# In the second batch, a pair's reciprocals copied in two parts, and the sums of w2's blocks placed behind masks and tallies

## The chip, the cores and the metric

The kernel runs on one core of one Trainium2 chip. The metric is device microseconds from start to end of one execution; the median of several runs is given. A profiled execution gives the trace from which all durations here are read.

## The reference, cut to what matters

Four batches of 768 positions. First comes attention of 8 heads of 64, in which a query sees only the keys whose six sign bits of a random projection agree with its own:

```python
q_bits = (einsum('bhsd,dk->bhsk', q, proj) > 0)      # and k_bits; a bucket number from six bits
mask   = q_bucket[..., None] == k_bucket[..., None, :]
scores = where(mask, scale * q @ k.T, -1e9)
attn   = softmax(scores);  x = attn @ v               # heads side by side: (4, 768, 512)
X = real(fft(fft(x, axis=1), axis=2));  u = x + X
un = (u - mean(u)) / sqrt(var(u) + 1e-6)
out = u + relu(un @ w_ch1) @ w_ch2                    # 512 -> 2048 -> 512
```

The weights come as 64-bit floats and are narrowed to 32 bits on the chip.

## The kernel before

The work is tiled by batch (b = 0 to 3). A batch has four pairs of heads; n counts pairs, so batch 1 has pairs 4 to 7. Each pair is done in six visits, one for each chunk c of 128 keys. In a visit, PE computes the chunk's scores in two halves of queries (L905, in two PSUM buffers that take turns), ACT exponentiates each half (`weights`, L916), DVE multiplies both heads by the 0/1 mask (`weigh`, L930, two instructions) and adds the chunk to a running sum (`tally`, L1020, one instruction in batch 1), and one visit later PE multiplies by v (`values`, L941). After a pair's last chunk `scale` divides: PE adds the tallies over keys (L960), DVE transposes the sums (L967), adds a small number and takes the reciprocal (L969, L970); ACT copies the reciprocals from 32-partition blocks into place, eight copies of 32x12 (L976); DVE transposes them out over the positions (L977) and multiplies x (L981). The generator `scale` stops (`yield`) after L970, and `attention` resumes it at the same visit or the next.

Beside the attention of batch b goes the rest of batch b - 1, as a second generator that `_main` advances between visits: `mix` (the Fourier part by folded matrices: `fold` L1099 to L1117, L1139, L1168, L1182) and then `mlp7`. The channel network is computed by a seven-product scheme on quarters of the matrices. Its inner part, for f = 0 to 7 in two halves, has seven products each (L1447); ACT copies or activates their PSUM banks (L1469, L1472, L1476, L1479, L1484, L1488, L1496, and L1486, L1490, L1498 in SBUF), DVE adds (L1473, L1480, L1485, L1489, L1497). Its outer part, `outer7`, once after each half, takes three pairs of row tiles with seven products each (L1326), whose banks are freed by DVE (L1338, L1372) or ACT (L1345, L1356, L1359). DVE prepares its left sides (L1311, L1312, L1346, L1354). Two PSUM banks in turn serve all these products, the bits (L836), the transposes (L1194) and the pairs' sums (L960).

In batch 0's channel network the weights are also still being made. `weights2` brings w2 in 16 slices, eight for each half of the network: a DMA on GpSimd's queue (L704), then `narrow`: DVE L639 and L643, ACT L647, L654, L655, DVE L652 twice. After each second slice DVE makes four sums of w2's blocks, each 128x256 (L1292 to L1295), which the outer products use beside the slices; SyncE's queue stores all seven blocks to DRAM (L1297) for later batches. For w1 the like is done by `quarters` (L1241 to L1244, stores at L1246 and L1247). SyncE's queue also carries the loads of q, k and v (L562, L568, L576) and of stored blocks (L1331, L1420).

The order on each engine is made by a scheduler from the program's order of tracing, with priorities and a model of times; it fixes each engine's queue at build time. Two tools in the code bend it: `behind()` puts a PE instruction behind a named one with higher priority, and `in_turn()` (a context of `_main`) puts all instructions traced inside it behind the instructions last noted in `done_by`, one for each engine. Noted are, for DVE, the masks L930, L1182 and some adds of the inner part, and for ACT the exponentials L916, L1146 and some of the inner part's copies. The conversion `arrival.convert` runs inside `in_turn()`, as does the tallying of batches 2 and 3 (`n >= TWO`, TWO = 8). The loop of visits for batches 0 and 1 is this, in short:

```python
new = chunk(c, scores(n, c)); tally(c, new[2], new[4])
for sc in scales: next(sc, None)          # then scales.clear()
while pending: finish()                   # values; after chunk 5, scale() up to its yield
for sc in scales if b else (): next(sc, None)
pending.append(new)
```

Of the kernel before, what the change touches and what calls it, by code (L numbers as in the profile page):

```python
# [17 lines left out]
ALU = mybir.AluOpType  # L18
# [8 lines left out]
NPAIR = H // 2  # L27
# [458 lines left out]
def _main(  # L486
# [13 lines left out]
    nc = tc.nc  # L500
# [13 lines left out]
    def wt(shape, dtype, tag, name, bufs=2):  # L514
        return work.tile(shape, dtype, tag=tag, name=name, bufs=bufs)
# [4 lines left out]
    def pt(shape, name):  # L520

        turn[0] += 1
        if roomy[0] and turn[0] % 2:
            if turn[0] % 4 == 1:
                return ps_o.tile(shape, F32, tag="o", name=name)
            return ps_sc.tile(shape, F32, tag="sc", name=name)
        return ps_1.tile(shape, F32, tag="ps", name=name)
# [152 lines left out]
    ET = mybir.EngineType  # L680
    done_by = {}

    @contextmanager
    def in_turn():

        with ExitStack() as st:
            for ins in done_by.values():
                st.enter_context(tc.issue_after(ins.ins))
            yield
# [186 lines left out]
    @contextmanager  # L876
    def behind():

        with tc.issue_after(last[0].ins), tc.high_priority(offset=AHEAD):
            yield  # L880

    TWO = 8
# [53 lines left out]
    def values(n, c, pk, oos):  # L936

        for g in range(2):
            w = HALF + 1 - g
            for h in range(2):  # L940
                oo = nc.tensor.matmul(  # L941
                    oos[g][h * D : (h + 1) * D, 0:w], nat["v", n][:, (2 * c + h) * D : (2 * c + h + 1) * D],
                    pk[:, g, h, 0:w], start=(c == 0), stop=(c == NT - 1),
                )
        last[0] = oo

    def scale(n, oos, sums):


        x = xs[n // NPAIR][:, n % NPAIR]  # L950
        vs = wt([P, 1], F32, "vs", f"vs{n}")
        nc.scalar.copy(vs, oos[0][:, HALF : HALF + 1])
        halves = [x[:, g * HALF : (g + 1) * HALF] for g in range(2)]
        for g, xg in enumerate(halves):
            nc.scalar.activation(xg, oos[g][:, 0:HALF], AF.Identity, bias=vs)

        ps = pt([P, HALF], f"sum{n}")
        for i, part in enumerate(sums):
            for j in range(4):
                nc.tensor.matmul(  # L960
                    ps[32 * j : 32 * j + 32, :], ones, part[:, j // 2, j % 2],
                    start=(i == 0), stop=(i == len(sums) - 1),
                )


        rt = wt([P, S], F32, "rt", f"rt{n}", 1)
        nc.vector.transpose(rt[:, 0:HALF], ps)  # L967
        rc = wt([P, HALF // 32], F32, "rc", f"rc{n}")
        nc.vector.tensor_scalar(rc, rt[:, 0:HALF:32], S * EPS, None, op0=ALU.add)  # L969
        nc.vector.reciprocal(rc, rc)  # L970
        yield
        rr = wt([P, 2, HALF // 32], F32, "rr", f"rr{n}")
        for g in range(2):
            for i in range(4):
                j = 2 * g + i // 2
                nc.scalar.copy(rr[32 * i : 32 * i + 32, g], rc[32 * j : 32 * j + 32])  # L976
        nc.vector.transpose(  # L977
            rt.rearrange("p (j i) -> p j i", i=32),
            rr.rearrange("p g j -> p (g j)")[:, :, None].broadcast_to([P, S // 32, 32]),
        )  # L980
        nc.vector.tensor_tensor(x, x, rt, op=ALU.mult)  # L981

    def attention(b):
        xs[b] = wt([P, NPAIR, S], F32, "x", f"x{b}")
        pending, scales = [], []

        def finish():
            n, c, pk, oos, sums = pending.pop(0)
            with behind() if n >= NPAIR and t is not None else nullcontext():
                values(n, c, pk, oos)  # L990
            if c == NT - 1:
                scales.append(scale(n, oos, sums))
                next(scales[-1])

        for t in range(NPAIR):
            n = NPAIR * b + t
            half = fold(b, 0) if t == NPAIR - 1 else iter(())
            if 1 < n + 1 < NPAIR * B:
                load(n + 1)
            ahead = prepare(n + 1) if n + 1 < NPAIR * B else iter(())  # L1000
            oos = [ps_o.tile([P, 512], F32, tag="o", name=f"oo{n}_{g}") for g in range(2)]
            acc = wt([P, 2, 2, HALF], F32, "acc", f"acc{n}", 1)
            first = None
            def chunk(c, pss):

                return n, c, weigh(n, c, pss), oos, [acc]

            def tally(c, pk, sums):

                nonlocal first  # L1010
                new = pk[:, :, :, 0:HALF]
                if c == 0:
                    first = new
                elif c == NT - 1 and b == 0:

                    sums.append(new)
                else:

                    for g in (0, 1) if b == 0 else (slice(0, 2),):
                        nc.vector.tensor_tensor(  # L1020
                            acc[:, g], (first if c == 1 else acc)[:, g], new[:, g],
                            op=ALU.add,
                        )

            for c in range(NT):
                if n < TWO:
                    new = chunk(c, scores(n, c))
                    tally(c, new[2], new[4])

                    for sc in scales:  # L1030
                        next(sc, None)
                    scales.clear()
                    while pending:
                        finish()
                    for sc in scales if b else ():
                        next(sc, None)
                    pending.append(new)
                elif c % 2 == 0:
                    pss = scores(n, c)
                    if len(pending) > 1:  # L1040
                        finish()
                    new = [chunk(c, pss)]
                    if pending:
                        finish()
                    new.append(chunk(c + 1, scores(n, c + 1, True)))
                    for sc in scales:
                        next(sc, None)
                    scales.clear()
                    pending += new
                else:  # L1050
                    with in_turn():
                        for p in pending:
                            tally(p[1], p[2], p[4])
                if c > (3 if b == 1 else 2):
                    next(half, None)
                if c > 0:
                    next(ahead, None)
                yield
        t = None
        while pending:  # L1060
            finish()
        for sc in scales:
            next(sc, None)


    HW = HALF // 2
# [199 lines left out]
    def weights2():  # L1266

        slices = []
        for half in range(2):
            for r in range(HF // 2):  # L1270
                for hi, first in ((0, B11), (1, B21)):
                    c = half * HF // 2 + r + hi * HF

                    step = 1 if hi else T1 - B11
                    dst = w2f[:, 0 : 7 * QB].rearrange("p (i r n) -> p i r n", i=7, n=HD)
                    slices.append(
                        (dst[:, first : first + step + 1 : step, r],
                         moe_w_ch2[c * P : (c + 1) * P, :])
                    )
        arrival = Arrival(slices, [zt2[:, i] for i in range(2)], NDC * DFF // WC, nc.gpsimd)  # L1280
        for half in range(2):
            if half == 0:
                for i in range(arrival.depth):
                    arrival.fetch(i)
                yield
            for i in range(HF):
                with in_turn():
                    arrival.convert(half * HF + i)
                yield
                if i % 2:  # L1290
                    b11, b21, b22, t4, t1, t2, t3 = (q[:, i // 2] for q in right7)
                    nc.vector.tensor_tensor(t3, b22, t1, op=ALU.subtract)  # L1292
                    nc.vector.tensor_tensor(t1, t1, b11, op=ALU.subtract)
                    nc.vector.tensor_tensor(t2, b22, t1, op=ALU.subtract)
                    nc.vector.tensor_tensor(t4, b21, t2, op=ALU.subtract)  # L1295
            for i in range(7):
                nc.sync.dma_start(bd[half, i], right7[i])  # L1297
            if half == 0:
                yield
# [350 lines left out]
```

## Time and profile before

| what | us |
|---|---|
| median of 3 runs | 1080.63 (1079.46 to 1081.03) |
| the profiled execution | 1081.91 |
| its span, first to last instruction | 1080.1 |
| PE busy | 1036.7 |
| DVE busy | 789.2 |
| ACT busy | 500.4 |
| exponentials L916, 192 of 809 ns | 147.4 busy |
| masks L930, 132 of 1014 ns | 128.7 busy |
| tallies L1020, 72 of 1485 ns on average | 106.0 busy |
| reciprocal copies L976, 128 of 198 ns (median) | 25 (128 x 0.198) |

The profiled execution's time is larger than its span by what lies ahead of the first and after the last instruction. In the trace's lines, the number in front is the start in us from the span's start, then the duration, the engine, the line of the kernel, the operation, what it writes and reads (buffer numbers left out), and shapes; the bracket at the end is the time in which the engine was idle before it and what ended that. A line can stand for several equal instructions that follow each other. PE's matmuls overlap, so a busy PE is not one at its peak; idle time of an engine that isn't the slowest costs nothing by itself. A stage is a stretch of the span for which the busy time of each engine was asked.

### The profile page before, as it was taken

To read this page: it belongs to the slowest core of one execution; us is meant where nothing else is said; L and a number is where in the kernel's file an instruction comes from. 1 tells how busy PE (TensorE), PEld (TensorE's weight loads), DVE (VectorE), ACT (ScalarE), POOL (GpSimd) and SP (SyncE) were. 2 spreads that over 40 slices of the span, in tenths; PEclk is the share of its full clock that TensorE was granted. 3 is DMA by queue.
4 is the path that set the end of the run, shared out by engine and by line. 5 is a ranking of instruction groups with operands and counts; after the bars stand their busy time and mean duration, and the time that the engine had idled before them with its cause. 6 is when DMAs were issued, how large, how long until landed. Compare 5 with 4: busy or idle time off the path is not lost.

```text
span 1080.1 us, 14131 instructions
## 1 busy us (share of the span) xinstructions
PE 1036.7 (96%) x4933; PEld 633.0 (59%) x4933; DVE 789.2 (73%) x1336; ACT 500.4 (46%) x1055; POOL 59.1 (5%) x132
## 2 busy tenths in 40 slices
PE   7989898999999999999999999999999999999997
PEld 3333354447644585545664576645675579668576
DVE  5899969888599977767857876776856875644353
ACT  6988554762277324455326424354315522440420
POOL 0000000002000020010000020010000012100000
PEclk9999899999999999999999999999999999999999
DMA  9654452390056271224062233222033205122301
GB/s 215 190 141 77 85 141 71 115 250 2 3 136 216 95 211 28 52 64 88 6 187 76 69 90 130 49 64 69 15 105 100 69 20 175 60 79 87 128 20 42
DMA packets 175710, 103.13 MB, mean 95 GB/s; under 512 B 129552, under 2 KB 162960, under 8 KB 175632
## 3 DMA queue, kind: packets, MB, share of 16 engines
q1 hardware_dynamic: 169840, 88.65, 30.5%
q0 software_dynamic: 4224, 13.11, 3.9%
q8 instruction: 41, 0.67, 0.3%
q10 hardware_dynamic: 1568, 0.39, 0.2%
q14 instruction: 37, 0.30, 0.1%
HBM read 81.14 MB, written 20.97 MB: 95 GB/s over the span
## 4 chain that ended last, share of the span: by engine, by line
PE 71%; DVE 17%; ACT 6%; issue 3%; SPq 2%; DMA 1%; DVEq 0%; ACTq 0%
PE o L1326 26%; PE h_p L1447 21%; PE oo L941 8%; PE sc L905 8%; DVE acc L1020 3%; DVE pk L930 3%; PE cs L1139 2%; PE A L1168 2%; ACT pk L916 2%; PE B L1168 1%; SPq L576 1%; DMA kn<-in_k_dram 1%; ACT rr L976 1%; DVE x L1182 1%; DVE w L643 1%
## 5 line engine op out<-in xcount | busy, mean ns | idle before, releaser
L1326 PE MATMUL o<-w,h 128*128 128x256 f32 x1152 | 258.4, 381 | 1.6 <-ACT tq L1345 0.9
L1326 PEld LDWEIGHTS o<-w,h 128*128 128x128 f32 x1152 | 216.7, 190 | 42.0 <-issue 6.4
L916 ACT ACTIVATE pk<-sc 128x768 f32<-128x768 f32 x192 | 147.4, 809 | 80.7 <-PE oo L941 33.2
L1447 PE MATMUL h_p<-x,w 128*128 128x384 f32 x448 | 164.1, 494 | 0.8 <-DVE rt L967 0.4
L905 PE MATMUL sc<-qt,kt 64*128 64x384 f32 x768 | 155.9, 508 | 3.6 <-ACT pk L916 3.3
L930 DVE SCALAR_TENSOR_TENSOR pk<-qb,kb,pk 128x768 f32<-128x768 bf16 x132 | 128.7, 1014 | 32.6 <-ACT pk L916 32.5
L941 PE MATMUL oo<-pk,vn 128*64 128x385 f32 (+1 forms) x768 | 146.8, 495 | 2.6 <-DVE pk L930 2.0
L1447 PEld LDWEIGHTS h_p<-x,w 128*128 128x128 f32 x448 | 82.0, 190 | 66.7 <-issue 9.9
L1020 DVE TENSOR_TENSOR acc<-acc,pk 128x1536 f32<-128x1536 f32 (+1 forms) x72 | 106.0, 1485 | 5.3 <-ACT pk L916 5.1
L1447 PE MATMUL h_p<-w 128*128 128x384 f32 x288 | 106.1, 490 | 0.1
L941 PEld LDWEIGHTS oo<-pk,vn 128*64 128x64 f32 x768 | 50.6, 136 | 88.9 <-issue 72.8
L905 PEld LDWEIGHTS sc<-qt,kt 64*128 64x128 f32 x768 | 67.0, 188 | 56.8 <-issue 20.6
L1447 PEld LDWEIGHTS h_p<-w 128*128 128x128 f32 x288 | 53.6, 190 | 39.6 <-ACT w L1484 2.4
L1338 DVE SCALAR_TENSOR_TENSOR w<-o,rs,w 128x256 f32<-128x256 f32 x56 | 26.7, 481 | 41.8 <-PE o L1326 41.8
L1356 ACT COPY tq<-o 128x256 f32<-128x256 f32 x24 | 9.0, 373 | 103.5 <-PE o L1326 103.5
L1326 PE MATMUL o<-w 128*128 128x256 f32 x176 | 42.2, 383 | 0.6 <-DVE w L1338 0.6
L1480 DVE TENSOR_TENSOR h<-h 128x384 f32<-128x384 f32 x32 | 17.8, 557 | 30.8 <-ACT h L1479 30.7
L1077 POOL DMA_DIRECT2D out_dram<-w x30 | 16.4, 548 | 402.7 <-issue 314.4
L1326 PEld LDWEIGHTS o<-w 128*128 128x128 f32 x176 | 32.9, 190 | 7.9 <-DVE w L1338 1.6
L1372 DVE TENSOR_TENSOR tq<-tq,o 128x256 f32<-128x256 f32 x24 | 10.1, 420 | 36.3 <-PE o L1326 36.3
L1473 DVE TENSOR_TENSOR h<-h 128x384 f32<-128x384 f32 x32 | 17.8, 555 | 23.7 <-ACT h L1472 23.7
L1345 ACT COPY tq<-o 128x256 f32<-128x256 f32 x24 | 8.9, 369 | 56.5 <-PE o L1326 56.3
(170 smaller groups left out, 1338.5 us busy)
## 6 DMA issues: line engine op xcount, KB each, us to landing
w<-ad SPq DMA_DIRECT2D x168, 128.0 KB, 2.0
w<-bd SPq DMA_DIRECT2D x42, 512.0 KB, 4.5
zraw<-in_moe_w_ch_dram POOLq DMA_DIRECT2D x16, 512.0 KB, 4.2
bd<-w SPq DMA_DIRECT2D x14, 512.0 KB, 3.6
vn<-in_v_dram SPq DMA_DIRECT2D x32, 192.0 KB, 3.4
qn<-in_q_dram SPq DMA_DIRECT2D x120, 48.0 KB, 2.4
kn<-in_k_dram SPq DMA_DIRECT2D x60, 96.0 KB, 3.0
zraw<-in_moe_w_ch_dram SPq DMA_DIRECT2D x8, 512.0 KB, 6.3
```

The lines of the kernel that those rows point to most:

```text
L905: last[0] = nc.tensor.matmul(ps[:, h, 0:HALF], kt[rows, ks], qt[rows, qs], start=kb is not None, stop=True,)
L916: done_by[ET.Activation] = nc.scalar.activation(pk[:, g, :, 0:HALF], ps[:, :, 0:HALF], AF.Exp, scale=SCALE)
L930: done_by[ET.DVE] = nc.vector.scalar_tensor_tensor(w, qb[:, h].rearrange("p (g s) -> p g s", g=2), kb[:, h, c : c + 1], w, op0=ALU.is_equa ...
L941: oo = nc.tensor.matmul(oos[g][h * D : (h + 1) * D, 0:w], nat["v", n][:, (2 * c + h) * D : (2 * c + h + 1) * D], pk[:, g, h, 0:w], start=( ...
L1020: nc.vector.tensor_tensor(acc[:, g], (first if c == 1 else acc)[:, g], new[:, g], op=ALU.add,)
L1139: nc.tensor.matmul(ps[:, pc + 2 * lo : pc + 2 * hi - 1 : 2], z[:, cp, pc, par, t * P : (t + 1) * P], ch[:, cp, pc, lo:hi], start=(cp == 0) ...
L1168: nc.tensor.matmul(ps[:, cols], F[:, par, k, t, j * P : (j + 1) * P], sq[:, t, k, cols], start=(t == 0), stop=(t == 1),)
L1326: nc.tensor.matmul(ps, a[:, r], right7[i][:, r], start=start and r == 0, stop=r == HF // 2 - 1, skip_group_check=not start,)
L1338: nc.vector.scalar_tensor_tensor(t[:, cols], src, r, t[:, cols], op0=ALU.mult, op1=ALU.add)
L1447: nc.tensor.matmul(ps, left[:, k], right[i][:, k], start=start and k == 0, stop=k == 1, skip_group_check=not start,)
L1473: done_by[ET.DVE] = nc.vector.tensor_tensor(c21, c12, c21, op=ALU.add)
L1480: done_by[ET.DVE] = nc.vector.tensor_tensor(c22, c21, c22, op=ALU.add)
```

## The change

There are three edits. First, for the pairs of batch 1 (`NPAIR <= n < TWO`), `scale` makes its eight copies in two parts of four, with a `yield` between them, each part inside `in_turn()`. In the loop above that places the second part (and the transpose and the product behind it) one visit later. At the end of a batch `attention` steps the last pair once, and if it stopped there, makes one more visit before the second step. Second, the tallies of all batches are noted in `done_by` for DVE, so that what runs inside `in_turn()` stands behind them too. Third, w2's four sums run inside `in_turn()`.

```diff
         rr = wt([P, 2, HALF // 32], F32, "rr", f"rr{n}")
+        apart = NPAIR <= n < TWO
         for g in range(2):
-            for i in range(4):
-                j = 2 * g + i // 2
-                nc.scalar.copy(rr[32 * i : 32 * i + 32, g], rc[32 * j : 32 * j + 32])
+            with in_turn() if apart else nullcontext():
+                for i in range(4):
+                    j = 2 * g + i // 2
+                    nc.scalar.copy(
+                        rr[32 * i : 32 * i + 32, g], rc[32 * j : 32 * j + 32]
+                    )
+            if apart and g == 0:
+                yield
         nc.vector.transpose(
...
                     for g in (0, 1) if b == 0 else (slice(0, 2),):
-                        nc.vector.tensor_tensor(
+                        done_by[ET.DVE] = nc.vector.tensor_tensor(
                             acc[:, g], (first if c == 1 else acc)[:, g], new[:, g],
...
         for sc in scales:
-            next(sc, None)
+            if next(sc, True) is None:
+                yield
+                next(sc, None)
...
                     b11, b21, b22, t4, t1, t2, t3 = (q[:, i // 2] for q in right7)
-                    nc.vector.tensor_tensor(t3, b22, t1, op=ALU.subtract)
-                    nc.vector.tensor_tensor(t1, t1, b11, op=ALU.subtract)
-                    nc.vector.tensor_tensor(t2, b22, t1, op=ALU.subtract)
-                    nc.vector.tensor_tensor(t4, b21, t2, op=ALU.subtract)
+                    with in_turn():
+                        nc.vector.tensor_tensor(t3, b22, t1, op=ALU.subtract)
+                        nc.vector.tensor_tensor(t1, t1, b11, op=ALU.subtract)
+                        nc.vector.tensor_tensor(t2, b22, t1, op=ALU.subtract)
+                        nc.vector.tensor_tensor(t4, b21, t2, op=ALU.subtract)
```

## The prediction

> **What bounds the kernel now.** I read the page first, then busy time by stages, then the timelines of TensorE (PE), ScalarE (ACT) and VectorE (DVE) in the stages that the edit reaches, and the queues of both built programs engine by engine. The page says PE:
>
> ```profile
> PE 1036.7 (96%) x4933; PEld 633.0 (59%) x4933; DVE 789.2 (73%) x1336; ACT 500.4 (46%) x1055; POOL 59.1 (5%) x132
> ```
>
> The built queues differ only where batch 1's attention runs beside batch 0's channel network, about 168 to 400 us; ahead of that and after it they are the same. By stages (stretch, length, then busy us of PE, PEld, DVE, ACT, POOL):
>
> ```profile
> 160.00:200.00 40.00, 35.75 (x154) 18.58 (x154) 35.91 (x61) 21.11 (x46) 1.34 (x3) 1.00 0.28 71
> 200.00:236.00 36.00, 35.84 (x145) 17.97 (x145) 33.27 (x67) 25.95 (x55) 2.65 (x5) 1.00 0.69 224
> 236.00:247.00 11.00, 8.66 (x40) 3.38 (x37) 9.37 (x15) 4.96 (x14) 1.53 (x4) 1.00 0.77 108
> 300.00:354.00 54.00, 50.98 (x202) 23.42 (x201) 51.60 (x99) 41.54 (x90) 3.27 (x6) 1.00 0.60 186
> 354.00:382.00 28.00, 25.81 (x122) 18.38 (x123) 27.11 (x54) 7.78 (x22) 2.65 (x5) 1.00 0.24 61
> ```
>
> See two things: PE is idle 4.25 + 0.16 + 2.34 + 3.02 + 2.19 = 12.0 us in these, all that the edit can win; and from 300 to 382 DVE is busy 78.7 of 82 us, so DVE sets the pace there. PE's idle pieces of the first stage, and of the stage at 240:
>
> ```profile
> 171.95 0.92 PE L1168 MATMUL B<-sq,F 128*128 128x193 f32 x4 [0.69 <-DVE rt L967]
> 174.49 0.92 PE L905 MATMUL sc<-qt,kt 64*128 64x384 f32 x4 [0.65 <-ACT pk L916]
> 176.88 0.92 PE L905 MATMUL sc<-qt,kt 64*128 64x384 f32 x4 [1.10 <-ACT pk L916]
> 181.04 1.51 PE L941 MATMUL oo<-pk,vn 128*64 128x385 f32 x4 [0.95 <-DVE pk L930]
> ...
> 242.26 0.92 PE L905 MATMUL sc<-qt,kt 64*128 64x384 f32 x4 [1.03 <-ACT pk L916]
> ...
> 245.13 1.51 PE L941 MATMUL oo<-pk,vn 128*64 128x385 f32 x6 [0.94 <-DVE pk L930]
> ```
>
> What stood ahead of the exponential (L916) there is ACT's eight reciprocal copies, 1.67 us:
>
> ```profile
> 239.70 1.67 ACT L976 COPY rr<-rc 32x12 f32<-32x12 f32 x8 [2.11 <-DVE mv L1202]
> 241.40 0.81 ACT L916 ACTIVATE pk<-sc 128x768 f32<-128x768 f32 x1
> ```
>
> And late, in the second outer stage, PE waits here:
>
> ```profile
> 356.49 3.82 PE L1326 MATMUL o<-w,h 128*128 128x256 f32 x16 [0.63 <-ACT w L1496]
> 360.92 1.99 PE L1326 MATMUL o<-w 128*128 128x256 f32 x8 [0.61 <-DVE w L1338]
> ...
> 378.05 1.99 PE L1326 MATMUL o<-w,h 128*128 128x256 f32 x8 [0.95 <-ACT tq L1345]
> ```
>
> **What the Trainium skill says.** "PSUM — Partial Sum Buffer", section Engine vs sequencer instructions: ScalarE's and VectorE's queues are strict FIFO, and matmuls start in program order. The trace agrees: the exponential at 241.40 starts 0.03 us after the eighth copy, though its scores ended at 236.9. So queue position is everything here. "Perfetto Trace Analysis", section Optimizing Scalar/DVE Operations: where these engines aren't saturated but leave bubbles on others, breaking work up may let it complete sooner. That fits 236 to 247 (ACT 45% busy) but not DVE after 300. "VectorE: DVE Perf Modes", section The TRN2 errata: a fixed cost per instruction, largest for small operands. The 32x12 copies agree, 198 ns each; the edit keeps their number, so it adds none.
>
> **The change part by part.** No arithmetic is added: copies, sums, masks and tallies keep their counts. I lay the new queues out with the old durations and pitches (mask L930 0.93, tally L1020 1.67, a 256-wide sum 0.34, L643 0.60, copy 0.21), each row starting at the later of its predecessor's end and its producer's end; a hand-over costs 0.03 to 0.1 us (L643 ends 320.55, L654 starts 320.58). A finer price of a hand-over is not in the trace; 0 to 0.1 over some dozen hand-overs on PE's way is 0 to 1 us, and I take about 0.05 each.
>
> *A, 168 to 236.* The first four w2 sums (169.60 to 171.32, 4 x 0.43) leave their place ahead of L967. It starts when the sum matmuls end, 170.1 instead of 171.3; PE's 0.69 goes, tally, exponentials and the second mask of the chunk follow 1.2 to 1.8 us earlier, and PE's score waits shrink with them. This pair's eight copies stay together in the built queue, so their split is worth 0 here. By 193 PE is 1.7 us ahead. The sums return between L1473 and L1480 of the first inner step, each later set likewise beside the next conversion. DVE then has no slack, and at 207 the bits threshold (L840) and the copy L1496 release PE only 1.0 early. By 234 I get 1.3 ahead. Bounds: 0 (all eaten by DVE) to 2.5.
>
> *B, 236 to 300.* The second pair's copies split into 4, exponential, 4. The exponential ends 1.55 us (what the reciprocal is ahead by) + 4 x 0.21 earlier; and the two masks now go ahead of the transpose L977 and the product L981 (0.91 + 0.87), so PE's last oo starts at 241.8, not 245.13: 3.3 ahead in all, 2.0 of it here. Given back: at the first outer products both masks of the next chunk stand before L1338, which frees a PSUM bank: PE waits 0.6 and 0.3 there. Ahead at 300: 3.3 - 0.9 = 2.4 us. From 247 to 300 PE was busy 53 of 53, so nothing else is won there; one visit's scores move from 254 to 271, at no cost since DVE has 15.6 us free.
>
> *C, 300 to 354.* Third pair. Its copies split too, but ACT puts L1498 ahead of the exponential and the masks stand ahead of the transpose: DVE idles 0.6 (308) and 2.2 (311 to 313.5) where it idled 1.4; later, masks placed before L1473 wait for their exponentials, 1.6 us near 342. DVE's own finish of this stretch, the add L1497, goes from 358.44 to 360.8: +2.4. PE gains 0.5 at L1484 (321.66) and later waits 1.1 for L1496 near 338, with the chunk's scores behind it; the first outer product goes from 353.87 to 354.25: +0.4. Bounds -1 to +2.
>
> *D, 354 to 400.* The last four w2 sums were finished at 349.7. Now they stand behind two masks, the fold's first add, a tally and L1480, L1485 and L1489, with L1104 between: L1489 ends at 355.9, the fourth sum 2.6 later, 358.5. The second product needs its block: it starts at 358.55, not 356.49: +2.06 in all. By the next bank the old wait of 0.61 is not repeated: +1.3 to +1.4 by the sum matmuls. Then two score chunks of batch 2 are put between products: the second one's second half needs the bank of an exponential that stands behind all eight copies of the last pair. The reciprocal (L970) ends at 378.6, copies to 380.3, exponential to 381.1, while PE is there at 378.9: 2.2 us of new idleness. Lag 3.65. The 0.95 at 378.05 (L1345 behind the copies) is gone, as it now stands ahead, and so is the 0.27 at 400.8: 3.65 - 1.2 = +2.4. Bounds 0 to +4.
>
> *Queues passed.* SP: the stores of w2's sums (bd) wait for the last sums, 6 to 9 us longer, with ring loads, pair 9's v and pair 10's q behind them. Pair 9's v waits anyway for the last oo of pair 7 (372.6), and q of pair 10 is first read at 386.95: cover of 14 us, cost 0; without it some us in D. POOL's raw fetches start when a conversion ends, which keeps its place: 0. The extra visit at the batch's end adds no work.
>
> Sum: -1.3 - 1.1 + 2.4 = 0.0 us, against the profiled span of 1080.1. That execution took 1081.91 in all, 1.8 more than its span and 1.3 above the runs' median of 1080.63; I put the sum on the median: 1080.6.
>
> **Rivals.**
> 1. *Faster.* A and B stand (-2.4), and DVE does not lose its 2.4 us in C, because exponentials come sooner than laid out. Then C keeps only its gain (-0.5); the fourth sum is on time and the 0.61 stays gone (-0.6); the reciprocal comes 2.4 us sooner and PE about 2, so the wait behind the copies is still 1.8; the old 0.95 + 0.27 go: D is 1.8 - 0.6 - 1.2 = 0.0. In all -2.9: 1077.7. For it: A and B remove waits that can be named. Against: DVE is 96% busy there and masks stand directly behind exponentials.
> 2. *Slower.* One mechanism: DVE idling behind ACT ahead of 350. Each us of it moves the fourth sum and the last reciprocal alike, and PE, already waiting for both, by 1 us. If A's 1.3 is eaten by DVE at 207 and the third pair's masks wait 1.4 longer, +2.7: 1083.3. It decides for slower by 0.2% when DVE's L1497 is over 4.6 us late to my 358.44 base, in place of 2.4. For it: three masks now stand ahead of work that is ready. Against: A's gain is on PE, not on DVE.
> That the edit does nothing is excluded by the queues; it does nothing only to the first pair's copies.
>
> **How the numbers follow.** Forecast 0.45, rival 1 0.27, rival 2 0.28. A measurement can tell about 0.2%, 2.2 us. Forecast: 0.37 within, 0.04 to each side; rival 1: 0.22 faster, 0.05 within; rival 2: 0.23 slower, 0.05 within. Faster 0.26, same 0.47, slower 0.27. The forecast's own range is 1078.6 to 1082.8; up to the rivals' values and a little of the bounds: 1077.3 to 1083.8.
>
> **What would show it.** Right: PE without the 0.69 at 172; an exponential between copies near 237, last oo of that stage 3 us early; a PE wait on the fourth sum before the second outer product; a PE score wait behind the last pair's copies; DVE's L1497 late against PE. Wrong: no lead at 247 (A, B), no wait at those two places (D), or any wait on q of pair 10 (SP).

## The result, and the profile after

The changed kernel takes 1078.06 us (median of 22 runs, 1077.37 to 1081.12), the kernel before 1080.68 (22 runs beside it, 1079.46 to 1081.39): ratio 0.998, 95% interval 0.9975 to 0.9986. That is about 0.2%, 2.6 us, faster, at the edge of what the forecast said can be told. The profiled execution took 1079.54 us with a span of 1077.8 (before: 1081.91 and 1080.1). The forecast was 1080.6. The time lies just outside the forecast's own range (1078.6 to 1082.8) and inside the wider one that takes in the rivals (1077.3 to 1083.8), near rival 1 (1077.7).

Lines of the changed kernel are numbered higher: the copies L976 are now L978, the transpose and product L977 and L981 are L983 and L987, tally L1020 is L1026, w1's sums L1242 and L1243 are L1250 and L1251, the mixing's L1182 and L1194 are L1190 and L1202, w2's four sums L1292 to L1295 are L1301 to L1304, their stores L1297 are L1306, outer products L1326 are L1335, the bank releases L1338 (DVE) and L1345 (ACT) are L1347 and L1354, inner products L1447 are L1456, and L1472, L1473, L1484, L1496, L1497, L1498 are L1481, L1482, L1493, L1505, L1506, L1507. All experiments have these numbers.

The busy times on the page of the changed kernel, and its stages (stretch, length, busy us of PE, PEld, DVE, ACT and POOL with counts, granted clock, DMA share, GB/s):

```profile
PE 1034.6 (96%) x4933; PEld 633.4 (59%) x4933; DVE 786.7 (73%) x1336; ACT 500.4 (46%) x1055; POOL 59.3 (5%) x132
```

```profile
160.00:200.00 40.00, 37.10 (x156) 19.57 (x153) 36.32 (x61) 21.81 (x47) 1.59 (x3) 1.00 0.29 79
...
236.00:247.00 11.00, 10.41 (x48) 6.46 (x48) 9.95 (x17) 6.18 (x16) 4.00 (x7) 1.00 0.70 173
...
300.00:354.00 54.00, 50.10 (x203) 24.62 (x200) 50.84 (x102) 40.64 (x89) 3.27 (x6) 1.00 0.53 163
354.00:382.00 28.00, 25.59 (x117) 16.73 (x116) 25.57 (x46) 9.10 (x21) 2.18 (x4) 0.94 0.39 104
```

PE's idle time falls from 4.25 to 2.90 us in the first of these stretches and from 2.34 to 0.59 between 236 and 247; from 300 to 354 it rises from 3.02 to 3.90. The clock of 0.94 in the last line is new and needs care. PE's idle pieces around the first two pairs, now:

```profile
171.92 0.52 PE L1202 MATMUL un<-ident,x 128*128 128x128 f32 x3 [0.72 <-DVE x L1190]
174.02 0.92 PE L905 MATMUL sc<-qt,kt 64*128 64x384 f32 x4 [0.48 <-ACT pk L916]
178.58 1.50 PE L941 MATMUL oo<-pk,vn 128*64 128x385 f32 x4 [0.29 <-DVE pk L930]
180.38 1.51 PE L941 MATMUL oo<-pk,vn 128*64 128x385 f32 x4 [0.29 <-DVE pk L930]
...
238.07 0.92 PE L905 MATMUL sc<-qt,kt 64*128 64x384 f32 x4 [0.19 <-ACT pk L916]
...
241.49 3.72 PE L1335 MATMUL o<-w,h 128*128 128x256 f32 x16
```

The 0.69 for L967 is gone, as forecast (a wait of 0.72 for L1190 stands near its place); 1.03 and 0.94 at 242 to 245 have become one of 0.19. ScalarE's timeline shows why, an exponential between two parts of four copies:

```profile
236.35 0.83 ACT L978 COPY rr<-rc 32x12 f32<-32x12 f32 x4 [1.96 <-DVE mv L1210]
237.21 0.81 ACT L916 ACTIVATE pk<-sc 128x768 f32<-128x768 f32 x1
238.04 0.82 ACT L978 COPY rr<-rc 32x12 f32<-32x12 f32 x4
```

And PE in the second outer stage:

```profile
350.39 5.01 PE L1335 MATMUL o<-w,h 128*128 128x256 f32 x22
355.34 1.56 PE L905 MATMUL sc<-qt,kt 64*128 64x384 f32 x8
...
361.25 5.45 PE L1335 MATMUL o<-w,h 128*128 128x256 f32 x24 [0.55 <-DVE w L1347]
...
372.61 0.92 PE L905 MATMUL sc<-qt,kt 64*128 64x384 f32 x4 [0.27 <-ACT pk L916]
375.11 1.05 PE L905 MATMUL sc<-qt,kt 64*128 64x384 f32 x4 [1.59 <-ACT pk L916]
376.09 5.23 PE L1335 MATMUL o<-w,h 128*128 128x256 f32 x16
```

There is no wait for the fourth sum: the first 22 matmuls, with the whole second product among them, follow each other. The waits behind the last pair's eight copies are there, 1.86 us. The last line shows something else: 16 matmuls that took 3.72 us at 241 take 5.23 here, because the granted clock was 0.60 on average between 376 and 380: the trace's record of it has 0.50 for 3.41 us from 375.77 on. Such dips lie at other places in other executions (the profile of before has them within 76 to 80 and 116 to 124), so two traces can't be compared by their starting times alone.

**How the traces are compared.** I follow six rows of PE that every kernel has, in before's time 159.82 (L1168), 237.13 (oo), 299.46 (inner product), 344.78 (scores), 371.16 (oo) and 406.05 (scores), and take start minus start in the profile of before, less the same difference at 159.82, up to which the queues are equal. Negative is ahead. For the changed kernel its second profile, without a dip there, is used. Where no dip lies between, two profiles of one kernel agree within 0.04 us (the changed kernel and sums_half0 have two each; the kernel before has one). From 406 to the end no difference moves by 0.1 us.

| kernel | 237 | 299 | 345 | 371 | 406 | ratio of the times, 95% interval |
|---|---|---|---|---|---|---|
| forecast | -1.3 | -2.4 | -2.0 (354) | -1.05 | 0.0 | |
| changed | -1.33 | -2.41 | -1.80 | -2.87 | -2.28 | 0.998, 0.9975 to 0.9986 |
| split_only | +0.53 d | -0.22 | -0.73 | -1.25 | -0.66 | 0.9984, 0.9977 to 0.999 |
| sums_only | -1.83 | -2.24 | -1.52 | -2.31 | -0.07 d | 0.9989, 0.9982 to 0.9996 |
| sums_half1 | -0.58 | -1.33 | -0.75 | -1.79 | +0.45 d | 1.0003, 0.9995 to 1.0011 |
| sums_half0 | -1.33 | -2.38 | -2.87 | -3.38 | -2.79 | 0.9969, 0.9958 to 0.998 |
| first_free | -1.32 | -2.39 | -2.83 | -2.53 | -1.94 | 0.9986, 0.9979 to 0.9992 |
| last_free | -1.35 | -2.42 | -1.78 | -3.12 | -3.15 | 0.9966, 0.9952 to 0.9979 |
| pair1_whole | -1.84 | -2.94 | -2.32 | -3.37 | -1.14 d | 0.9977, 0.9969 to 0.9985 |
| pair2_whole | -1.33 | -1.78 | -1.16 | -2.23 | -1.64 | 0.999, 0.9982 to 0.9999 |
| pair3_whole | -1.33 | -2.41 | -1.73 | -2.52 | -1.93 | 0.9987, 0.9979 to 0.9995 |
| combined | -1.84 | -2.92 | -2.31 | -3.65 | -3.67 | 0.9964, 0.995 to 0.9977 |

A "d" marks a dip of the clock since the column before. What one costs is read from the changed kernel, whose first profile stands at -0.60 at 406 where the second has -2.28: 1.68 us, nearly what half the clock takes in 3.41 us.

### The profile page after: what moved, and what is told of

The parts are those of the page before. It is cut to its first block, busy times and chain, and to the rows that moved or that the text cites. A ratio compares the mean times of both kernels' runs of the same rounds, so it can differ in the third digit from the quotient of the medians.

```text
span 1077.8 us, 14130 instructions
## 1 busy us (share of the span) xinstructions
PE 1034.6 (96%) x4933; PEld 633.4 (59%) x4933; DVE 786.7 (73%) x1336; ACT 500.4 (46%) x1055; POOL 59.3 (5%) x132
## 4 chain that ended last, share of the span: by engine, by line
PE 72%; DVE 17%; ACT 6%; issue 2%; DMA 1%; SPq 1%; DVEq 0%; ACTq 0%
PE o L1335 26%; PE h_p L1456 22%; PE oo L941 8%; PE sc L905 7%; DVE acc L1026 3%; DVE pk L930 2%; PE cs L1147 2%; ACT pk L916 2%; PE A L1176 2%; PE B L1176 1%; DMA kn<-in_k_dram 1%; ACT rr L978 1%; DVE x L1190 1%; PE sum L960 1%; SPq L576 1%
## 5 line engine op out<-in xcount | busy, mean ns | idle before, releaser
L1335 PE MATMUL o<-w,h 128*128 128x256 f32 x1152 | 260.0, 383 | 0.8 <-DVE w L1347 0.6
L1335 PEld LDWEIGHTS o<-w,h 128*128 128x128 f32 x1152 | 217.8, 191 | 41.8 <-issue 6.5
L1456 PE MATMUL h_p<-x,w 128*128 128x384 f32 x448 | 164.5, 494 | 3.1 <-ACT h L1478 1.6
L1456 PEld LDWEIGHTS h_p<-x,w 128*128 128x128 f32 x448 | 82.0, 190 | 69.3 <-issue 9.9
L1026 DVE TENSOR_TENSOR acc<-acc,pk 128x1536 f32<-128x1536 f32 (+1 forms) x72 | 105.8, 1483 | 5.3 <-ACT pk L916 5.1
L1456 PE MATMUL h_p<-w 128*128 128x384 f32 x288 | 106.1, 490 | 0.1
L1456 PEld LDWEIGHTS h_p<-w 128*128 128x128 f32 x288 | 53.6, 190 | 39.6 <-ACT w L1493 2.4
L1347 DVE SCALAR_TENSOR_TENSOR w<-o,rs,w 128x256 f32<-128x256 f32 x56 | 26.6, 479 | 41.2 <-PE o L1335 41.2
L1335 PE MATMUL o<-w 128*128 128x256 f32 x176 | 42.2, 383 | 0.2 <-DVE w L1347 0.2
L1335 PEld LDWEIGHTS o<-w 128*128 128x128 f32 x176 | 32.9, 190 | 7.5 <-DVE w L1347 1.2
L1354 ACT COPY tq<-o 128x256 f32<-128x256 f32 x24 | 8.8, 368 | 60.3 <-PE o L1335 60.1
L1482 DVE TENSOR_TENSOR h<-h 128x384 f32<-128x384 f32 x32 | 17.7, 552 | 21.8 <-ACT h L1481 21.7
```

Of the source, the lines that this page charges most:

```text
L1026: done_by[ET.DVE] = nc.vector.tensor_tensor(acc[:, g], (first if c == 1 else acc)[:, g], new[:, g], op=ALU.add,)
L1335: nc.tensor.matmul(ps, a[:, r], right7[i][:, r], start=start and r == 0, stop=r == HF // 2 - 1, skip_group_check=not start,)
L1347: nc.vector.scalar_tensor_tensor(t[:, cols], src, r, t[:, cols], op0=ALU.mult, op1=ALU.add)
L1456: nc.tensor.matmul(ps, left[:, k], right[i][:, k], start=start and k == 0, stop=k == 1, skip_group_check=not start,)
L1482: done_by[ET.DVE] = nc.vector.tensor_tensor(c21, c12, c21, op=ALU.add)
```

## The experiments

Every edit is to the changed kernel. First the two edits each alone, and the sums' edit by halves of the network.

**split_only.** The second and third edit taken back (the third makes the sums' `in_turn()` a `nullcontext()`).

```diff
-                        done_by[ET.DVE] = nc.vector.tensor_tensor(
+                        nc.vector.tensor_tensor(
...
-                    with in_turn():
+                    with nullcontext():
                         nc.vector.tensor_tensor(t3, b22, t1, op=ALU.subtract)
```

> Only the copies in two parts; w2's sums and the tallies as before. Theory P (each edit acts in its own place, and the places add up): nothing at 172; the waits of 1.03 and 0.94 us at 242 to 245 go, 0.4 is given back at the first outer products, the third pair costs 0.6; the last pair's copies stand 4, bank copy, 4, so that the wait of 0.95 at 378 shrinks to 0.1, and no scores of batch 2 are put ahead of the products: about -2.2 us, 1078.4. Theory Q (the two edits work only together, the lead made at 172 is what carries): 0 to -0.6 us, 1080 to 1080.7.

Measured 1078.64 us (21 runs) beside 1080.40. A dip at 172 to 180 hides the first step; after it PE wins 0.75 by 299, 0.51 by 345, 0.52 by 371 and loses 0.59 by 406. The split is worth something alone, so the two edits don't need each other; theory Q is out. Theory P has nearly the total (1.8 us for its 2.2) but not the parts: from 299 to 345 it expected a cost of 0.6, where 0.51 is won.

**sums_only.** The split and the tally's note taken back.

```diff
-        apart = NPAIR <= n < TWO
+        apart = False
```

> Only w2's sums behind masks and tallies; all pairs' copies in eights. Theory P: 0.69 at 172 and most of the exponential waits after it go, lead 1.3 to 1.6 us at 236; the waits at 242 to 245 stay or shrink by the lead of the exponentials; scores of batch 2 ahead of products wait about 1.6 to 1.9 us behind the last pair's eight copies, against 1.2 of old waits gone: about -0.8 us, 1079.9. Theory Q: 0 to -0.4 us, 1080.3 to 1080.7.

Measured 1078.81 (20 runs). The lead at 237 is 1.83 us, more than with both edits. 1.02 and 0.94 at 238 to 242 stay. At 406 it would be -1.75 without the dip, so the expected 0.8 us of gain was too small. The gains of the two alone add up to more than the whole (1.8 and 1.6 against 2.6 us), so they overlap.

**The tallies' note** was not run: with it or without it, with both other edits or with neither, all built queues are the same row for row. It does nothing here.

**sums_half0 and sums_half1.** The sums' edit in one half of the network only.

```diff
-                    with in_turn():
+                    with in_turn() if half == 0 else nullcontext():    # sums_half0
+                    with in_turn() if half else nullcontext():         # sums_half1
```

> The changed kernel with w2's sums placed behind masks and tallies for the first four sets only; the last four sets lie as in the kernel before. The queues are the changed kernel's up to about 330, then the last pair's copies stand 4, bank copy, 4 and the scores of batch 2 after the outer products. Theory P: the 1.86 us of score waits behind the last pair's copies are real loss; they go, 0.1 + 0.27 of the old waits come back: -1.5 us against the changed kernel, 1076.6. Theory R (DVE sets the pace there, and the time lost behind the copies would be lost at the next bank anyway): no change against the changed kernel, 1078.1.

> The changed kernel with w2's sums placed behind masks and tallies for the last four sets only. Up to 236 the queues are those of before, from there those of the changed kernel. Theory P: the lead of 1.3 to 1.6 us at 236 is missing and nothing else changes: 1079.5. Theory S (what is won at 172 is lost again at the next wait on DVE, the pace of 236 to 350 is DVE's): no change against the changed kernel, 1078.1.

sums_half0 took 1077.33 (7 runs), and as half0_again 1076.97 (7 runs): by the medians 0.7 and 0.8 us faster than the changed kernel, though the intervals overlap, and 0.5 by the traces. That is half of what theory P gave or less. Its trace says why. The waits behind the copies are gone, but from 371 to 406 it loses 0.59 us like the changed kernel, to other waits:

```profile
372.27 1.99 PE L1335 MATMUL o<-w,h 128*128 128x256 f32 x8 [0.27 <-ACT tq L1354]
374.50 1.99 PE L1335 MATMUL o<-w,w 128*128 128x256 f32 x8 [0.23 <-DVE u L1347]
376.75 10.63 PE L1335 MATMUL o<-w,h 128*128 128x256 f32 x48 [0.26 <-DVE w L1347]
```

For this kernel theory R is right at this place: between 371 and 406, PE loses no more with 1.86 us of score waits than with these. (last_free, below, does not agree.) sums_half0's gain lies ahead: it leads the changed kernel by 1.07 us at 345, and still by 0.51 at 371.

sums_half1 took 1080.39 (13 runs, up to 1084.26). Its VectorE queue is not that of before up to 236, as was expected: the first pair's transpose and product stand elsewhere already, at 176.9 and 178.7, behind w1's sums and not among them. Its lead at 237 is 0.58 instead of 1.33; the difference of 0.75 is 1.08 by 299, and still 1.08 at 371, as theory P has it: the lead made ahead of 237 is kept. By its trace it should be about 1.2 us faster than before when the dip is taken off; the times show nothing. The runs have part of the answer. In the three of its runs with a mean clock of 0.997 or more the median span is 1077.2 us, in 34 such runs of the kernel before 1078.3: the gain is there, as far as three runs can tell. Against it stand more time outside the span (median 2.40 us, before 1.96) and lower clocks (10 of 13 runs under 0.997, before 16 of 50). Why these are so stays open.

**first_free and last_free.** In the second half, the sets of sums are at i = 1, 3, 5, 7. With the first set bound, the built queues are the same whether 3 and 5 are bound or not, so last_free differs from the changed kernel in the last set alone, and from sums_half0 in the first alone. With the first free they are not: first_free differs from the changed kernel in the first set alone, but from sums_half0 in 3, 5 and 7.

```diff
-                    with in_turn():
+                    with in_turn() if half == 0 or i > 1 else nullcontext():    # first_free
+                    with in_turn() if half == 0 or i < 7 else nullcontext():    # last_free
```

> The changed kernel, but the first set of w2's sums of the second half (the four at 314.3 to 316.6 in the changed kernel) is not placed behind masks and tallies, so that it lies at 302 to 307 as in the kernel before; TensorE's queue is the changed kernel's, row for row. Theory F (sums that are ready fill VectorE's time behind ScalarE; forbidding that is what costs between 300 and 345): VectorE's idle time near 304 and 307 falls from 2.6 to about 1.4 us, TensorE loses 0 or gains 0.5 us from 300 to 345 instead of losing 0.63, total 1077.2 to 1077.5. Theory G (the split of the third pair's copies costs there): TensorE still loses 0.6 us from 300 to 345, total 1078.1.

> The changed kernel, but the last set of w2's sums (the four at 350.4 to 352.6) is not placed behind masks and tallies. The scores of batch 2 then stand behind the outer products, and the last pair's eight copies stand behind the bank copy. Theory F: the first set is still forbidden, so that 300 to 345 still costs 0.6 us; no wait for scores of batch 2 at 372 to 375, about 0.5 us gone after 371, and the granted clock of 376 to 380 stays at 1.00: 1077.5. Theory R: the waits come back as waits on DVE at the next banks, total as the changed kernel's, 1078.1. A late fourth sum, as the forecast had it, would show as a gain of 0.5 us or more between 345 and 371.

first_free took 1078.58 (21 runs), last_free 1077.22 (5 runs). VectorE's idle pieces of the changed kernel between 300 and 345:

```profile
304.10 1.95 DVE L930 SCALAR_TENSOR_TENSOR pk<-qb,kb,pk 128x768 f32<-128x768 bf16 x2 [0.45 <-ACT vs L952]
309.46 1.95 DVE L930 SCALAR_TENSOR_TENSOR pk<-qb,kb,pk 128x768 f32<-128x768 bf16 x2 [2.13 <-ACT pk L916]
...
344.45 1.95 DVE L930 SCALAR_TENSOR_TENSOR pk<-qb,kb,pk 128x768 f32<-128x768 bf16 x2 [0.32 <-ACT pk L916]
```

and those of first_free:

```profile
309.49 1.95 DVE L930 SCALAR_TENSOR_TENSOR pk<-qb,kb,pk 128x768 f32<-128x768 bf16 x2 [1.41 <-ACT pk L916]
321.80 0.56 DVE L1506 TENSOR_TENSOR h<-h,w 128x384 f32<-128x384 f32 x1 [0.34 <-ACT w L1505]
337.92 1.95 DVE L930 SCALAR_TENSOR_TENSOR pk<-qb,kb,pk 128x768 f32<-128x768 bf16 x2 [0.66 <-ACT pk L916]
344.97 1.95 DVE L930 SCALAR_TENSOR_TENSOR pk<-qb,kb,pk 128x768 f32<-128x768 bf16 x2 [0.54 <-ACT pk L916]
```

The first set, free, fills the time near 304 to 309 (2.58 us idle become 1.41), and PE wins 0.44 us from 299 to 345 instead of losing 0.61. Most of the difference falls at one wait of the changed kernel, for a sum of w1's blocks on VectorE, which first_free does not have:

```profile
337.58 1.53 PE L1456 MATMUL h_p<-bt,tq 128*128 128x384 f32 x4 [1.25 <-DVE tq L1250]
```

So far theory F. But its total fails: first_free is not faster than the changed kernel. By the pieces shown VectorE idles as long in both (2.95 and 2.90 us), only later, and from 345 on, where both have the same order, its rows are 0.34 us later than in the changed kernel. PE's lead of 1.03 us over the changed kernel is handed back at once, to banks:

```profile
351.93 3.62 PE L1335 MATMUL o<-w,h 128*128 128x256 f32 x14 [0.27 <-ACT w L1505]
...
361.77 5.45 PE L1335 MATMUL o<-w,h 128*128 128x256 f32 x24 [0.93 <-DVE w L1347]
```

At 371 PE too is 0.34 us behind the changed kernel.

last_free shows the contrary: nothing won by 345, but 1.34 us from 345 to 371 (changed: 1.07), where the wait at the bank of L1347 is absent, and no loss after 371 (changed: 0.59):

```profile
356.59 0.70 PE L1335 MATMUL o<-w,h 128*128 128x256 f32 x2 [0.26 <-ACT h L1507]
371.78 3.72 PE L1335 MATMUL o<-w,h 128*128 128x256 f32 x16 [0.29 <-DVE rt L967]
375.86 1.99 PE L1335 MATMUL o<-w,w 128*128 128x256 f32 x8 [0.37 <-DVE u L1347]
```

At 406 binding the last set costs 0.87 us (-3.15 to -2.28), and binding 3, 5 and 7 with the first set free costs as much (-2.81, the second profile of sums_half0, to -1.94); binding the first set wins 0.34 in both pairs. The gain at 345 that looked decisive was not. The places of the 0.87 differ: beside last_free, 0.25 of it falls ahead of 371 and 0.62 behind, where the changed kernel's PE waits for scores; beside sums_half0 all of it falls ahead of 371. So the score waits do cost in one pair and not in the other.

**changed_again and half0_again.** The same two kernels, for second profiles.

> The changed kernel once more, for a second profile and for times beside the others. If the dip of the granted clock at 376 to 380 follows from TensorE's waits of 0.27 and 1.59 us before it, it is there again, and the time is 1078.1; if it was chance, the clock there is 1.00.

> The kernel with the first half's sums alone behind masks and tallies, once more. 1077.3 and no dip of the clock at 376 to 380; if the dip falls by chance, it is as likely here as in the changed kernel.

changed_again took 1077.76 (8 runs; 0.9978, 0.9968 to 0.9989). The waits are as before, 0.27 and 1.59, but the clock did not dip. The stretch from 376 to 380 in the first profile of the changed kernel (the clock is the third number from the end):

```profile
376.00:380.00 4.00, 4.00 (x13) 3.23 (x12) 3.23 (x5) 0.81 (x1) 0.00 (x0) 0.60 0.57 91
```

and in its second:

```profile
376.00:380.00 4.00, 4.00 (x20) 3.52 (x19) 4.00 (x6) 0.81 (x1) 0.00 (x0) 1.00 0.65 104
```

So the dip is not a fixed consequence of the wait. Of the eight profiles with this wait (1.59 or 1.60 us) four have a dip right after it (the changed kernel's first, sums_only, sums_half1, pair1_whole); of the six without it, before's among them, none has one there. But the same four are the only ones of the eight with a dip near 116 to 124 as well, and in all four the late dip begins 259.4 us after that one began. An early dip alone is not enough either: before and last_free have it, without the wait, and no late one. The runs' mean clocks, which don't tell where a dip lies, were 0.995 or less in 46 of 125 runs of the kernels with this wait, in 4 of 45 of the variants without it, and in 29 of 124 of the kernel before. The late dip came where both the wait and the early dip were; what brings it is open.

**pair1_whole, pair2_whole, pair3_whole.** One pair's copies in one part.

```diff
-        apart = NPAIR <= n < TWO
+        apart = n in (5, 6, 7)    # pair1_whole; (4, 6, 7) pair2_whole; (4, 5, 7) pair3_whole
```

> The changed kernel, but the first pair's copies (and the transpose and product behind them) are not made in two visits. The forecast took this split as worth 0: TensorE's lead at 237 stays 1.3 us, total 1078.0. Theory A (places add up): in the kernel with the sums' edit alone the lead at 237 was 1.8 us, in that with the split alone it was 0.6, so the two overlap and the first pair's split takes 0.5 back: lead 1.8 at 237, total 1077.4 to 1077.5.

> The changed kernel, but the second pair's copies are not made in two visits; the queues differ from the changed kernel's only between about 234 and 260, and in a few places of VectorE's after 360. Theory A: the waits of 1.03 and 0.94 us at 238 to 242 come back, from 237 to 300 TensorE wins 0.4 instead of 1.1 us: 1078.7. Theory W (the order at the first outer products gives back what the split wins, so that it is worth nothing): 1078.0.

> The changed kernel, but the third pair's copies are not made in two visits; the queues differ from the changed kernel's only between about 302 and 345. The forecast charged the loss from 300 to 354 to this split: without it TensorE wins 0.4 us there, 1077.6. Theory F (the loss comes from the second half's sums, which can no longer fill VectorE's time): from 300 to 345 still 0.6 us lost, 1078.0.

pair1_whole, 1078.24 (15 runs), can't be told from the changed kernel by its times; its trace leads by 1.84 at 237 instead of 1.33, as theory A had it. The forecast overlooked what the first pair's second visit moves. VectorE in the changed kernel:

```profile
176.65 0.97 DVE L983 STREAM_TRANSPOSE rt<-rr 128x768 f32<-128x768 f32 x1
177.55 0.98 DVE L930 SCALAR_TENSOR_TENSOR pk<-qb,kb,pk 128x768 f32<-128x768 bf16 x1
178.44 0.95 DVE L987 TENSOR_TENSOR x<-x,rt 128x768 f32<-128x768 f32 x1
179.31 1.94 DVE L930 SCALAR_TENSOR_TENSOR pk<-qb,kb,pk 128x768 f32<-128x768 bf16 x2
```

and in pair1_whole, whose start lies 0.70 us later (the row at 171.92 is at 172.62):

```profile
173.86 0.98 DVE L983 STREAM_TRANSPOSE rt<-rr 128x768 f32<-128x768 f32 x1
...
175.07 0.95 DVE L987 TENSOR_TENSOR x<-x,rt 128x768 f32<-128x768 f32 x1
...
179.21 2.87 DVE L930 SCALAR_TENSOR_TENSOR pk<-qb,kb,pk 128x768 f32<-128x768 bf16 x3
```

The eight copies stand together in both, but in the changed kernel the transpose and the product behind them were pushed between masks. On PE, two of the four matmuls of an inner product then stand behind the values that wait for these masks (L1456 at 181.82, after two waits of 0.29); in pair1_whole all four stand ahead, at 178.08, and one wait of 0.64 follows. In step with 159.82, PE is 0.5 us earlier in pair1_whole from there on, and VectorE 0.52 from 201 to 400. Alone (sums_half1) the first pair's split goes with a lead of 0.58; beside the sums' edit it takes 0.5 back. That is the overlap ahead of 237: 1.83 and 0.58 alone, 1.33 together.

pair2_whole, 1079.35 (13 runs), brings back the three waits of before:

```profile
238.39 0.92 PE L905 MATMUL sc<-qt,kt 64*128 64x384 f32 x4 [1.03 <-ACT pk L916]
239.47 0.86 PE L941 MATMUL oo<-pk,vn 128*64 128x385 f32 x2 [0.16 <-DVE pk L930]
...
241.27 1.51 PE L941 MATMUL oo<-pk,vn 128*64 128x385 f32 x6 [0.94 <-DVE pk L930]
```

From 237 to 299 it wins 0.45 instead of 1.08: the second pair's split is worth 0.63, and the difference stays to the end. pair3_whole, 1079.29 (13 runs), still loses 0.68 from 299 to 345 and wins 0.79 from 345 to 371 instead of 1.07: the loss between 300 and 345 is not the third pair's split, which is worth 0.3.

**combined.** last_free and pair1_whole together.

```diff
-        apart = NPAIR <= n < TWO
+        apart = NPAIR < n < TWO
...
-                    with in_turn():
+                    with in_turn() if half == 0 or i < 7 else nullcontext():
```

> Both better variants at once: the last set of w2's sums not placed behind masks and tallies, and the first pair's copies not made in two visits; the rest as in the changed kernel. Theory A (places add up): TensorE is ahead of the kernel before by 1.8 us at 237, 2.9 at 300, 2.3 at 345, 3.6 at 371 and at the end: about 1077.0. Theory W (the time from 300 to 361 is VectorE's own, so that TensorE's extra 0.5 us is waited away at the bank that VectorE frees near 361): 3.1 at the end as without the second edit, 1077.4.

Measured 1076.71 (5 runs) beside 1081.26: 0.9964 (0.995 to 0.9977), the fastest of all. PE stands at -3.67 at 406, -3.6 was expected from adding up the places; theory W is out. Against sums_half0 and last_free the intervals overlap.

## Why the forecast was right in its wider range only, and wrong in its sum

**A (168 to 236), right in size.** 1.33 ahead, 1.3 forecast, with the squeeze that it expected after 193 (0.81 for L1505 at 205.94, and 1.12 at 197.44). Its claim that the first pair's split is worth 0 was wrong, by 0.5 us against, and the sums' edit alone is worth 1.83. So the agreement is luck: two misses of 0.5 us cancel.

**B (236 to 300), right.** 1.08 won, 1.1 forecast, and in its parts too. The row behind the last values was, before,

```profile
246.57 5.64 PE L1326 MATMUL o<-w,h 128*128 128x256 f32 x24
```

and starts at 241.49 now: with the offset of 1.70 it is 3.38 ahead, 3.3 forecast. By 299 0.97 of that is given back, 0.9 forecast. The two waits at the first outer products are listed with 0.19 and 0.23 of idle time, where 0.6 and 0.3 were forecast, but cost 0.27 and 0.38 by the starts of the rows, and the first is ended by ScalarE's bank copy (L1354), not by L1347; the rest goes in small pieces by 277. The waits vanish with the second pair's split and come back without it. The Trainium skill's "Perfetto Trace Analysis", section Optimizing Scalar/DVE Operations, says that breaking up instructions may help where an engine that isn't saturated leaves bubbles on others; here the eight copies stayed whole and their run was broken up, to the same effect.

**C (300 to 354), right for PE's sum, wrong for DVE.** PE loses 0.6, 0.4 forecast. The gain at L1484 came (PE is 0.45 us further ahead there than at 299, 0.5 forecast); the wait near 338 is 1.25 us for 1.1, but for w1's sum L1250 on DVE and not for the bank copy L1496. Of DVE's three idle pieces two came as laid out (0.45 and 2.13; 0.6 and 2.2 forecast), the third, 1.6 near 342, shrank to 0.32. The add on DVE, before and now:

```profile
358.44 0.56 DVE L1497 TENSOR_TENSOR h<-h,w 128x384 f32<-128x384 f32 x1
...
360.38 0.49 DVE L1338 SCALAR_TENSOR_TENSOR w<-o,rs,w 128x256 f32<-128x256 f32 x1
```

```profile
352.56 0.42 DVE L1304 TENSOR_TENSOR w<-w 128x256 f32<-128x256 f32 x1
...
354.72 0.55 DVE L1506 TENSOR_TENSOR h<-h,w 128x384 f32<-128x384 f32 x1
355.19 0.48 DVE L1347 SCALAR_TENSOR_TENSOR w<-o,rs,w 128x256 f32<-128x256 f32 x1
```

L1506 starts at 354.72, 3.72 us earlier than L1497 did. In step with PE's lead of 2.40, and with the offset of 1.70, it would be 4.10 earlier: it is 0.4 late, not 2.4.

**D (354 to 400), where it failed.** The step is: "The second product needs its block: it starts at 358.55, not 356.49: +2.06 in all." From 299 to 371 PE should have lost 1.35 us and won 0.46. Two things were wrong. The fourth sum ends at 352.98 (L1304 starts at 352.56), on the forecast's axis 352.98 + 1.70 + 2.40 = 357.1 and not 358.5, because the third idle piece was missing. And the last set makes only the last of the four slices that a product reads: for the second product that is matmul 15 of the row that starts at 350.39, at a pitch of 4.95/22 = 0.225 us reached at 353.5, over 0.5 us after the sum. So nothing waited. What PE won besides is the old pair of waits, 0.63 and 0.61, for one of 0.55: L1505 is 5.08 ahead of its old start where PE is 3.48 (353.87 to 350.39), and L1347 follows L1506 by 0.47 us (355.19 after 354.72) where L1338 followed L1497 by 1.94. Binding the last set does cost, 0.87 us beside last_free, but at the bank behind it (0.25) and after 371 (0.62), not at the sum.

The second half of D was right in mechanism and a little large: score waits of 1.86 where 2.2 was forecast, 0.95 and 0.27 gone, +0.59 from 371 to 406 where about +1.0 was forecast. Whether this wait is a cost of its own depends on what it is compared with: sums_half0, which doesn't have it, loses the same 0.59; last_free, which doesn't have it either, loses nothing.

**Queues passed, right in cost.** SyncE stores the last blocks by 353.84 (before: 351.39, so with the offset 4 us later and not 6 to 9) and loads v and q of the later pairs in time; PE waits for neither. SyncE's issues in the changed kernel:

```profile
343.83 10.01 SPq L1306 DMA_DIRECT2D bd<-w  x6
...
368.51 1.02 SPq L562 DMA_DIRECT2D vn<-in_v_dram  x2
369.58 0.53 SPq L576 DMA_DIRECT2D qn<-in_q_dram  x1
```

So rival 1 came closest: DVE did not lose its 2.4 us, and the fourth sum was on time. But its own sum, -2.4 - 0.5 + 0.0, got C's sign wrong (0.6 was lost) and misses D's gain (0.5): that its total is near the 2.3 us of the traces is luck in part.

## What to carry to other kernels

When an operation is bound to a later place, ask which part of its consumer reads it: here only the last quarter did, and a late sum cost nothing at its reader. A lead won ahead of a stretch that another engine paces was worth here what that engine also gained: first_free's 1.03 us at 345 was gone at 371, where VectorE was 0.34 us late; the 0.5 us of pair1_whole, which VectorE had too, stayed. Follow the buffer releases (here the add that frees a bank), not the nearest wait, and don't call a gain real before the next release is passed. And when instructions are moved by a generator's extra stop, count everything behind the stop, not only the instructions that the edit names.

## What the runs showed of the hardware

PE's granted clock fell to 0.50 for 3.41 us, or twice that, in some executions and not in others of the same kernel, at changing places; one such dip cost 1.68 us. (From 1069 to 1076 us on, close to the end, it is at 0.50 in all 14 profiles.) With effects of 1 to 3 us a single profile misleads: at 159.82, up to which the queues are the same, the profile of before stands 1.70 us behind the changed kernel's first one and 1.58 behind its second. The first of the three has dips at 76 and 117, the second one at 116 and the third none, so that the dips alone do not account for these offsets either. And a PE wait costs more than its listed idle time: the row at 356.49 in the kernel before starts 0.82 us after 353.87 + 8 x 0.225 (353.87 is the start of the first outer product there, 0.225 the pitch found above), with 0.63 listed.
